# Smaller copies of the split values, and spare time ahead of four norm products, in a fused attention and MoE kernel

## The chip, the core and the metric

The kernel runs on one core of a Trainium2 chip. Times are device microseconds of one execution on that core. TensorE is called PE, VectorE DVE, ScalarE ACT, GpSimd POOL and SyncE SP, as in the profile. SP computes nothing here; it issues the copies and transposes that this text speaks of.

## The reference

Causal block attention, then two feed-forward stages without biases, all on float32 inputs.

```
B, H, S, D = 4, 8, 576, 64
scores = (q @ k.T) / sqrt(D)                   # per head
scores = where(i // 64 >= j // 64, scores, -1e9)
attn = softmax(scores)                         # with 1e-9 added to the sum
x = (attn @ v) as [2304, 512]

a, b = x @ w1, x @ w2                          # [2304, 1024]
x = ((a * b) @ w3) @ w_out                     # [2304, 512]

r = maximum(x @ w_in, 0)                       # [2304, 2048]
out = (r * r) @ w_out2
```

## The kernel before

Float32 products are made of 16-bit ones: an operand is split into an upper part (fp16, "h") and a remainder (fp16, "l"), and three products stand for one. Other operands (g, w3·w_out, the later q and k) are split into two fp32r parts in the same way.

**Attention** works on pairs of heads, p = 0 to 15, two heads on the two halves of the 128 partitions, and on query tiles t = 0 to 4 in three groups g. For each group the scores go to a PSUM buffer `s` (L917 on PE; pairs 3 to 7 in float32 on `kraw,qraw`, later ones on split `qk`), DVE takes the row maxima `nm` (L951, L959), ACT the exponentials `pf` (L976), DVE the reciprocals `r`, and ACT and DVE the split weights `p` (L1020, L1027). SP then transposes `p` into `pt` by DMA (L1037). `attend` multiplies `pt` with the values in two parts (`attend 0` and `attend 1` of a pair, L1112) and ACT and DVE split the result into `x..h` and `x..l` (L1128, L1133).

Causality comes in blocks of 64 keys. So `attend` needs the values not only as `split_v` makes them (`v16`, five blocks of 128 keys) but also shifted by 64 keys (`vsh`) and with blocks that are mixed from two (`vmix`). Both are copies from SBUF to SBUF that SP issues (L863), four for each pair from pair 3 on: `mixb` 0, `mixb` 1, `s0`, `s1`. The shifted copies hold upper and lower parts; `attend` reads their upper parts alone (`for hl in range(1 if w is sh else 2)`).

**The first MoE stage** follows batch by batch behind attention and fills PE between its steps. `ab_products` (L1208) makes a and b from x in 12 products for each of 8 tiles f of w1/w2, ACT scales a (L1363), DVE multiplies (L1370), and g = a·b is split. `y_products` multiplies g with the product w3·w_out; ACT evicts y (`ys`, L1413) and POOL stores it. ab and y take turns in three PSUM banks of 512 columns, so an ab product may wait until ACT has evicted the y that had its bank.

w1/w2's eight tiles f are converted from 64-bit words and scaled by a power of two before they are split: `w12_tile` sums squares of each half on ACT (`junk`, L431) or takes maxima on DVE (`wsum`, L424), `norm_scale` multiplies these sums by a matrix of ones on PE to spread them over all partitions (L375, a product of 2 columns into `pv_bank`), and DVE makes the scale's exponent from that (L381, L283) for the split (L302, L305). The same helper serves two other norms, with n = 1.

**The second MoE stage** (from about 500 us on) uses Strassen's products on split operands; no line of it is changed.

**Order.** Nothing of this is issued where it is written. Each step is recorded with an engine, a modelled cost, what it reads and writes, a key and a spare time:

```
def op(self, eng, cost, fn, r=(), w=(), key=0.0, spare=0.0):
```

`emit` then plans the whole program: on each engine it takes the step that can start earliest, and of those that can start by then the one with the smallest key. A step can start when its producers are done by the model; from another engine that is

```
u.ready = max(u.ready, free[eng] + u.same if same else o.end + self.WAIT + u.spare)
```

So `spare` holds a step back in the plan: others pass it. A DMA's cost is a triple: 0.6 us of issue on SP or POOL, its length in KB times 0.0033 us in one shared pipe, and 4.0 us until it has landed:

```
def c_dma(kb):
    return (0.6, kb * 0.0033, LATE)
```

The plan is fixed when the program is built. On the chip each engine works through its own queue in the planned order and waits on semaphores for what is really done.

Of the kernel before, what the change touches and what calls it, by code (L numbers as in the profile page):

```python
# [10 lines left out]
F16 = mybir.dt.float16  # L11
# [3 lines left out]
AF = mybir.ActivationFunctionType  # L15
ALU = mybir.AluOpType
# [3 lines left out]
P = 128  # L20
# [9 lines left out]
NTILE = 5  # L30
# [50 lines left out]
class Order:  # L81
# [14 lines left out]
    def buf(self, pool, tag, bufs, shape, dtype, name):  # L96
        b = Buf(self, pool, tag, bufs, shape, dtype, name)
        self.bufs.append(b)
        return b
# [88 lines left out]
def fused_kernel(ctx: ExitStack, tc: tile.TileContext, qT, kT, vp, va, w12, w3t, wo, wb, out):  # L188
    nc = tc.nc
    act, dve, pe, sp, pool = nc.scalar, nc.vector, nc.tensor, nc.sync, nc.gpsimd  # L190
    ctx.enter_context(tc.manual_schedule())

    od = Order()
    buf = od.buf

    PE, ACT, DVE, SQ, GQ = "P", "A", "V", "S", "G"
# [16 lines left out]
    def c_dma(kb):  # L213
        return (0.6, kb * 0.0033, LATE)
# [154 lines left out]
    def norm_scale(n, col, sums, sum_keys, scale, inverse, key):  # L369


        bank = norm_cols[0]
        od.op(
            PE, 0.06,
            lambda: pe.matmul(bank()[:, NB + col : NB + col + n], upper(ones, 0, P), upper(sums, 0, n), start=True, stop=True),  # L375
            [(ones,)] + sum_keys, [(bank, col)], key,
        )
        h = at_buf("nh", 2, [P, 2], I32, f"nh_{col}")
        od.op(
            DVE, c_dve(8),  # L380
            lambda: dve.tensor_scalar(  # L381
                out=h()[:, :n], in0=bank().bitcast(I32)[:, NB + col : NB + col + n], scalar1=24, scalar2=None,
                op0=ALU.logical_shift_right,
            ),
            [(bank, col)], [(h,)], key,
        )
        od.op(DVE, c_dve(8), lambda: bits(scale(), h()[:, :n], -1.0, 204.0), [(h,)], [scale.key], key)
        od.op(DVE, c_dve(8), lambda: bits(inverse(), h()[:, :n], 1.0, 50.0), [(h,)], [inverse.key], key)
# [181 lines left out]
    def at_buf(tag, bufs, shape, dtype, name):  # L570
        return buf("at", tag, bufs, shape, dtype, name)
# [11 lines left out]
    vals = {}  # L583
# [217 lines left out]
    def split_v(p):  # L801

        key = 2 * p * HEAD + 2
        src = raws[p][2]
        first = p < KDM
        one = p < 2 * KDM
        sc = None if one else vsc[2 * p // H][0]
        t = at_buf("vraw" if first else "v16", 2, [P, NTILE, 2, P], F16, f"v16_{p}")  # L810
        wide = (NTILE + NTILE - 1) * 2 * P
        if first:
            slot = (5, 6)[p - KDM]
            mixb = sh_ = buf("base", f"w8_{slot}", 1, [P, wide], F16, f"vmix_{p}")
        else:
            mixb = buf("cv", "raw", RAW_BUFS, [P, 512], I64, f"vmix_{p}")
            sh_ = buf("cv", "cx", 2, [P, NTILE - 1, 2, P], F16, f"vsh_{p}")

        def mix():
            m = mixb() if first else mixb().bitcast(F16)  # L820
            return m[:, : NTILE * 2 * P].rearrange("p (c h x) -> p c h x", c=NTILE, h=2)

        def sh():
            if not first:
                return sh_()
            return sh_()[:, NTILE * 2 * P :].rearrange("p (c h x) -> p c h x", c=NTILE - 1, h=2)

        if one:
            sx = x_scale[2 * p // H][0]

            def joined_heads():
                return src().rearrange("p c a d -> p c (a d)")

            split_scaled(
                lambda: t()[:, :, 0, :], lambda: t()[:, :, 1, :], joined_heads, 640,
                ([(t, "h", a) for a in range(2)], [(t, "l", a) for a in range(2)], [(src,)]), (sx, [sx.key]), key,
            )
        for a in range(0 if one else 2):
            n = (2 * p + a) % H
            cols = slice(D * a, D * a + D)  # L840
            od.op(
                ACT, c_act(320),
                lambda a=a, n=n, cols=cols: act.activation(
                    t()[:, :, 0, cols], src()[:, :, a, :], AF.Copy, scale=sc()[:, n : n + 1]
                ),
                [(src,), (sc,)], [(t, "h", a)], key,
            )
            od.op(
                DVE, c_dve(320),
                lambda a=a, n=n, cols=cols: dve.scalar_tensor_tensor(  # L850
                    out=t()[:, :, 1, cols], in0=src()[:, :, a, :], scalar=sc()[:, n : n + 1],
                    in1=t()[:, :, 0, cols], op0=ALU.mult, op1=ALU.subtract,
                ),
                [(src,), (sc,), (t, "h", a)], [(t, "l", a)], key,
            )
        whole = [(t, x, a) for x in "hl" for a in range(2)]
        for w, o, i in (
            ((mixb, 0), lambda: mix()[0:64], lambda: t()[0:64]),
            ((mixb, 1), lambda: mix()[64:128], lambda: t()[0:64, 0:1].broadcast_to([64, NTILE, 2, P])),
            ((sh_, "s0"), lambda: sh()[0:64], lambda: t()[64:128, : NTILE - 1]),  # L860
            ((sh_, "s1"), lambda: sh()[64:128], lambda: t()[0:64, 1:]),
        ):
            od.op(SQ, c_dma(190), lambda o=o, i=i: sp.dma_start(out=o(), in_=i()), whole, [w], key)  # L863
        vals[p] = t, mix, sh, whole + [(mixb, 0), (mixb, 1), (sh_, "s0"), (sh_, "s1")]

    def pair(p):

# [207 lines left out]
    def attend(p, part):  # L1075

        b = 2 * p // H
        key = (2 * p + 1) * HEAD + 6 + part
        c0, gn = GS[part]
        pv = pv_bank[0]  # L1080
        if whole(p):
            attend_whole(p, part, pv)
            return
        v, mix, sh, v_keys = vals[p]
        lo_t, hi_t = PARTS[part]
        todo = []
        for kind, w in ((0, v), (1, sh)):
            for c in range(hi_t):
                tiles = [t for t in (lo_t, hi_t) if c < t]
                if GROUP_OF[lo_t] == GROUP_OF[hi_t]:  # L1090
                    todo.append((w, c, tiles, [PT_BASE[t] + c + kind * (t + 1) for t in tiles]))
                else:
                    todo += [(w, c, [t], [PT_BASE[t] + c + kind * (t + 1)]) for t in tiles]
        todo += [(mix, t, [t], [PT_BASE[t] + t]) for t in (lo_t, hi_t)]
        if part == 0:
            todo.append((mix, 0, [0], [PT_BASE[0]]))
        steps = [(w, c, tiles, o, hl) for w, c, tiles, o in todo for hl in range(1 if w is sh else 2)]

        def products(lo, hi):
            for n in range(lo, hi):  # L1100
                w, c, tiles, o, hl = steps[n]
                for a in range(2):
                    pt = pts[2 * p + a, GROUP_OF[tiles[0]]]
                    rows = slice(64 * a, 64 * a + 64)
                    nq = 64 if tiles == [0] else 128
                    dst = pv()[rows, q_start(tiles[0]) - c0 : q_start(tiles[-1]) + nq - c0]
                    if len(tiles) == 2:
                        dst = dst.rearrange("p (t x) -> p t x", x=P)
                        rhs = pt()[:, o[0] : o[1] + 1 : o[1] - o[0], :]
                    else:  # L1110
                        rhs = pt()[:, o[0], :nq]
                    pe.matmul(dst, w()[:, c, hl, rows], rhs, start=n == 0, stop=n == len(steps) - 1)  # L1112

        pt_ks = [k for a in range(2) for g in ((0, 1) if part == 0 else (1, 2)) for k in pt_keys[2 * p + a, g]]
        cost = sum(c_mm(128 * len(s[2])) for s in steps)
        od.op(PE, cost + 0.2, lambda: products(0, len(steps)), v_keys + pt_ks, [(pv, "pv")], key, spare(p))
        xh, xl = x_part(p, part)
        kc = p % KDM
        if b > 1:
            t_back = vsc[b][1]  # L1120
            backs = [(t_back, 0), (t_back, 1)]

        def back():
            return t_back()[:, kc : kc + 1] if b > 1 else 2.0**-PEXP

        od.op(
            ACT, c_act(gn, 0.05),
            lambda: act.activation(xh(), pv()[:, :gn], AF.Copy, scale=back()),  # L1128
            [(pv, "pv")] + (backs if b > 1 else []), [(xh,)], key,
        )  # L1130
        od.op(
            DVE, c_dve(gn, 0.06),
            lambda: dve.scalar_tensor_tensor(  # L1133
                out=xl(), in0=pv()[:, :gn], scalar=back(), in1=xh(),
                op0=ALU.mult, op1=ALU.subtract,
            ),
            [(pv, "pv"), (xh,)] + (backs if b > 1 else []), [(xl,)], key,
        )
# [1323 lines left out]
```

## Time and profile before

| | |
|---|---|
| median of 3 runs | 834.83 us (833.37 to 835.41) |
| the profiled execution's own time | 834.87 us |
| its span, first to last instruction | 833.1 us |
| granted TensorE clock, mean | 0.997 of full speed |
| PE, weight load on PE, DVE, ACT, POOL busy | 815.8, 661.4, 707.3, 612.4, 103.4 us |

Busy is the union of an engine's instructions. PE's weight loads overlap its products. The span leaves out what lies before the first and behind the last instruction, 1.77 us of the execution's time.

### The profile page before, as it was taken

Reading aid. Unit: us, or ns where it says so; the run is one execution under the profiler, and the core shown is the slowest. Engines: PE = TensorE matmul, PEld = TensorE weight load, DVE = VectorE, ACT = ScalarE, POOL = GpSimd, SP = SyncE. Lnnn points to the kernel's source line nnn. Section 1 sums busy time; section 2 is a strip of 40 time slices with the busy share of each in tenths; the row PEclk is TensorE's granted clock in tenths of the full one; section 3 lists DMA queues with packets and bytes.
Section 4 is the critical chain, followed back from the end, with each engine's and each line's share of the span. In section 5 each row is a group of like instructions: output and inputs, shape, how many; then the busy total and the mean of one; then the engine's idle time right before and its main releaser. Section 6 shows DMA issues by size and latency. Waiting matters only on the chain.

```text
span 833.1 us, 18899 instructions
## 1 busy us (share of the span) xinstructions
PE 815.8 (98%) x7282; PEld 661.4 (79%) x7286; DVE 707.3 (85%) x1640; ACT 612.4 (74%) x1399; POOL 103.4 (12%) x190
## 2 busy tenths in 40 slices
PE   8999999999999999999999999999999999999997
PEld 7456777789779898798879887666678888888886
DVE  5999889988888998837787889999979898787775
ACT  5999988966886888847999967575756655673652
POOL 5021110112111012011313101100020000001000
PEclk9999999999999999999999999999999999999999
DMA  8856757789998899664746401120030011001001
GB/s 331 323 205 189 171 153 162 184 178 236 189 184 176 169 181 198 130 129 136 238 142 234 152 15 64 53 75 2 1 127 1 2 39 39 2 1 52 1 2 52
DMA packets 111739, 102.42 MB, mean 123 GB/s; under 512 B 89440, under 2 KB 93600, under 8 KB 110240
## 3 DMA queue, kind: packets, MB, share of 16 engines
q0 software_dynamic: 17888, 71.18, 26.3%
q1 hardware_dynamic: 93760, 30.03, 20.1%
q8 instruction: 57, 0.93, 0.5%
q14 instruction: 34, 0.28, 0.1%
HBM read 62.78 MB, written 9.44 MB: 87 GB/s over the span
## 4 chain that ended last, share of the span: by engine, by line
PE 52%; DVE 10%; ACT 4%; issue 1%; DVEq 0%; ACTq 0%
PE p L1987 14%; PE ab L1208 13%; PE p L2155 11%; PE y L1208 6%; PE o L2282 5%; PE pv_bank L1112 2%; PE s L917 1%; DVE t L2110 1%; DVE s L1930 1%; DVE c L2019 1%; ACT c L2050 1%; DVE g L295 1%; ACT c L2053 1%; DVE gs L295 1%; DVE ts L2132 1%
## 5 line engine op out<-in xcount | busy, mean ns | idle before, releaser
L1208 PEld LDWEIGHTS <-w 128*128 128x128 f16 x1536 | 147.0, 98 | 43.7 <-issue 6.8
L976 ACT ACTIVATE pf<-s,nm 128x192 f32<-128x192 f32 (+4 forms) x160 | 83.3, 536 | 38.5 <-DVE nm L959 33.0
L1208 PE MATMUL ab<-x0h,w 128*128 128x320 f16 x512 | 109.8, 299 | 0.7 <-ACT ys L1413 0.7
L1208 PE MATMUL y<-g,w3o 128*128 128x320 f32 (+1 forms) x768 | 109.5, 299 | 0.0
L1208 PEld LDWEIGHTS y<-g,w3o 128*128 128x128 f32 x768 | 103.3, 188 | 2.0 <-issue 1.1
L1208 PE MATMUL ab<-x1h,w 128*128 128x256 f16 x512 | 88.1, 273 | 1.3 <-ACT ys L1413 1.3
L2155 PEld LDWEIGHTS <-gs 128*128 128x128 f16 x816 | 79.5, 98 | 10.4 <-DVE gs L295 1.3
L1987 PEld LDWEIGHTS <-wb 128*128 128x128 f16 x768 | 75.1, 98 | 12.1 <-issue 0.5
L1208 PE MATMUL ab<-x0l,w 128*128 128x320 f16 x256 | 76.5, 299 | 0.0
L1027 DVE SCALAR_TENSOR_TENSOR p<-pf,r,p 128x192 f16<-128x192 f32 (+4 forms) x130 | 67.4, 546 | 4.4 <-ACT p L1020 3.7
L1208 PE MATMUL ab<-x1l,w 128*128 128x256 f16 x256 | 69.8, 272 | 0.0
L1020 ACT ACTIVATE p<-pf,r 128x192 f16<-128x192 f32 (+4 forms) x130 | 67.3, 569 | 1.9 <-DVE r L993 1.2
L2282 PE MATMUL o<-wb,g 128*128 128x512 f16 x288 | 66.3, 379 | 0.3 <-DVE c L2292 0.2
L2050 ACT ACTIVATE c<-c,beta 128x512 f32<-128x512 f32 x48 | 34.3, 714 | 43.5 <-DVE c L2019 43.5
L1987 PEld LDWEIGHTS <-st 128*128 128x128 f16 x576 | 56.3, 98 | 7.2 <-issue 0.3
L2155 PE MATMUL p<-ts,gs 128*128 128x256 f16 x480 | 61.6, 273 | 0.1
L2282 PEld LDWEIGHTS <-g 128*128 128x128 f16 x288 | 28.0, 98 | 30.0 <-issue 0.5
L2155 PE MATMUL p<-wb,gs 128*128 128x256 f16 x336 | 44.7, 273 | 0.1
L293 ACT ACTIVATE gs<-c 128x512 f16<-128x512 f32 (+1 forms) x56 | 29.9, 535 | 18.3 <-DVE c L2061 18.1
L951 DVE TENSOR_REDUCE nm<-s 128x2 f32<-128x384 f32 (+1 forms) x64 | 42.1, 684 | 1.0
L356 DVE CUSTOM_DVE_ANT_0 cx<-raw,cx 128x1024 uint16<-128x1024 uint16 (+1 forms) x53 | 39.1, 738 | 2.9 <-ACT raw L347 0.7
L261 ACT ACTIVATE g<-a 128x320 fp32r<-128x320 f32 (+1 forms) x64 | 28.2, 441 | 16.0 <-DVE a L1370 15.5
(287 smaller groups left out, 1988.7 us busy)
## 6 DMA issues: line engine op xcount, KB each, us to landing
raw<-in_wb POOLq DMA_DIRECT2D x32, 512.0 KB, 5.5
raw<-in_w3t POOLq DMA_DIRECT2D x8, 1024.0 KB, 10.1
raw<-in_w POOLq DMA_DIRECT2D x16, 512.0 KB, 4.9
yraw<-ydram POOLq DMA_DIRECT2D x12, 512.0 KB, 4.2
vraw<-in_vp POOLq DMA_DIRECT2D x16, 320.0 KB, 4.7
qraw<-in_qT POOLq DMA_DIRECT2D x16, 288.0 KB, 4.0
kraw<-in_kT POOLq DMA_DIRECT2D x16, 288.0 KB, 5.1
vmix<-v SPq DMA_DIRECT2D x26, 160.0 KB, 4.8
```

The lines of the kernel that those rows point to most:

```text
L261: od.op(ACT, c_act(n), lambda: act.activation(hi(), src(), AF.Copy), [ks], kh, key)
L293: od.op(ACT, c_act(n), lambda: act.activation(hi(), src(), AF.Copy), ks, kh, key)
L356: dve.tensor_tensor(out=x(), in0=x(), in1=words()[1], op=ALU.add)
L951: lambda k=k, t=t, nm=nm, banks=banks: dve.tensor_reduce(out=nm()[:, k], in_=banks[0]()[:, :, S_COL[t] : S_COL[t] + n_keys(t)], op=ALU.max ...
L976: act.activation(o, view(a, t), AF.Exp, bias=nm()[:, k, a : a + 1], scale=SCALE, accum_out=ssum()[:, k, a : a + 1],)
L1020: lambda o=o, nk=nk, a=a, k=k, w=weights, p16=p16, r=r: act.activation(p16()[:, o : o + nk], w(a, k), AF.Copy, scale=r()[:, k, a : a + 1]),
L1027: lambda o=o, nk=nk, a=a, k=k, w=weights, p16=p16, r=r: dve.scalar_tensor_tensor(out=p16()[:, o + nk : o + 2 * nk], in0=w(a, k), scalar=r( ...
L1208: pe.matmul(acc(), l, r, start=k == 0, stop=k == len(mms) - 1)
L1987: pe.matmul(acc()[:, TH * half : TH * half + TH], lhs(a, kc), y[yn]()[:, kc], start=n == 0, stop=n == len(mms) - 1,)
L2050: lambda src=src, k=k: act.activation(src(), src(), AF.Relu, scale=beta()[:, j, k : k + 1]),
L2155: pe.matmul(acc()[:, TH * u : TH * u + TH], t()[:, o : o + P], r(b), start=first and n == 0 and u == tiles[0], stop=last and n == 2 and u ...
L2282: pe.matmul(o(), g[gx]()[:, cols], wt(f)[:, a, 512:1024], start=(begin and n == 0), stop=(last and n == 2),)
```

## The change

Two edits. The first is in `split_v` and in the two places that read its tiles. The split values `v16` are laid out as upper half, then lower half, instead of block by block; the shifted copies `vsh` hold the upper half alone (64 KB each instead of 128); the second mixed copy is issued in two (upper 80 KB, lower 80 KB). The shifted copies and one of the mixed ones need only the upper parts of v to be done. Where each of four copies was planned with 190 KB, the five are planned with 64, 64, 160, 80 and 80, and the shifted ones come first. The second edit gives `norm_scale`'s product a spare of 1.1 us where n is 2 and col at least 8, that is for tiles f = 4 to 7 of w1/w2.

```
 def norm_scale(n, col, sums, sum_keys, scale, inverse, key):
...
-            [(ones,)] + sum_keys, [(bank, col)], key,
+            [(ones,)] + sum_keys, [(bank, col)], key, 1.1 * (n == 2 and col >= 8),
...
 def split_v(p):
...
-        t = at_buf("vraw" if first else "v16", 2, [P, NTILE, 2, P], F16, f"v16_{p}")
-        wide = (NTILE + NTILE - 1) * 2 * P
+        t = at_buf("vraw" if first else "v16", 2, [P, 2, NTILE, P], F16, f"v16_{p}")
+        wide = (3 * NTILE - 1) * P
...
-            sh_ = buf("cv", "cx", 2, [P, NTILE - 1, 2, P], F16, f"vsh_{p}")
+            sh_ = buf("cv", "cx", 2, [P, NTILE - 1, P], F16, f"vsh_{p}")
...
-            return m[:, : NTILE * 2 * P].rearrange("p (c h x) -> p c h x", c=NTILE, h=2)
+            return m[:, : NTILE * 2 * P].rearrange("p (h c x) -> p h c x", h=2, c=NTILE)
...
         whole = [(t, x, a) for x in "hl" for a in range(2)]
-        for w, o, i in (
-            ((mixb, 0), lambda: mix()[0:64], lambda: t()[0:64]),
-            ((mixb, 1), lambda: mix()[64:128], lambda: t()[0:64, 0:1].broadcast_to([64, NTILE, 2, P])),
-            ((sh_, "s0"), lambda: sh()[0:64], lambda: t()[64:128, : NTILE - 1]),
-            ((sh_, "s1"), lambda: sh()[64:128], lambda: t()[0:64, 1:]),
+        upper_ = [(t, "h", a) for a in range(2)]
+        for w, o, i, kb, ks in (
+            ((sh_, "s0"), lambda: sh()[0:64], lambda: t()[64:128, 0, : NTILE - 1], 64, upper_),
+            ((sh_, "s1"), lambda: sh()[64:128], lambda: t()[0:64, 0, 1:], 64, upper_),
+            ((mixb, 0), lambda: mix()[0:64], lambda: t()[0:64], 160, whole),
+            ((mixb, 1), lambda: mix()[64:128, 0], lambda: t()[0:64, 0, 0:1].broadcast_to([64, NTILE, P]), 80, upper_),
+            ((mixb, 2), lambda: mix()[64:128, 1], lambda: t()[0:64, 1, 0:1].broadcast_to([64, NTILE, P]), 80, whole),
         ):
-            od.op(SQ, c_dma(190), lambda o=o, i=i: sp.dma_start(out=o(), in_=i()), whole, [w], key)
+            od.op(SQ, c_dma(kb), lambda o=o, i=i: sp.dma_start(out=o(), in_=i()), ks, [w], key)
...
-                    pe.matmul(dst, w()[:, c, hl, rows], rhs, start=n == 0, stop=n == len(steps) - 1)
+                    x = w()[:, c, rows] if w is sh else w()[:, hl, c, rows]
+                    pe.matmul(dst, x, rhs, start=n == 0, stop=n == len(steps) - 1)
```

The plan is made anew from these costs, so most of the order behind the first changed copy moves a little. PE has 11768 rows in either program; SP has 122 before and 128 now, one row standing for two equal issues where they follow each other. Line numbers behind the edit are 2 or 3 higher in the changed kernel.

On PE, at the sums of w1/w2's last tile (`wsum_7`), the end of one ab group, the norm product, and the scores of pair 5's last group stood so before:

```order
L1208 MATMUL ab_0_0_6_0_2056<-x0h3_0_1351,w12_3_1959 128x320
L375 LDWEIGHTS ones_89
L375 MATMUL pv_bank_356<-wsum_7_2064,ones_89 128x2
L917 MATMUL s_5_2_0_2087<-kraw_5_1223,qraw_5_1216 128x288
L917 MATMUL s_5_2_1_2089<-kraw_5_1223,qraw_5_1216 128x288
L917 MATMUL s_5_2_0_2087<-kraw_5_1223,qraw_5_1216 128x288
L917 MATMUL s_5_2_1_2089<-kraw_5_1223,qraw_5_1216 128x288
L1208 LDWEIGHTS w12_3_1959
L1208 MATMUL ab_0_0_6_1_2106<-x0h0_0_461,w12_3_1959 128x320
```

and stand so now:

```order
L1211 MATMUL ab_0_0_6_0_2059<-x0h3_0_1352,w12_3_1975 128x320
L919 MATMUL s_5_2_0_2087<-kraw_5_1224,qraw_5_1217 128x288
L919 MATMUL s_5_2_1_2089<-kraw_5_1224,qraw_5_1217 128x288
L919 MATMUL s_5_2_0_2087<-kraw_5_1224,qraw_5_1217 128x288
L919 MATMUL s_5_2_1_2089<-kraw_5_1224,qraw_5_1217 128x288
L375 LDWEIGHTS ones_89
L375 MATMUL pv_bank_356<-wsum_7_2067,ones_89 128x2
L1211 LDWEIGHTS w12_3_1975
L1211 MATMUL ab_0_0_6_1_2103<-x0h0_0_461,w12_3_1975 128x320
```

The norm product has moved behind the four rows of scores (eight products, a row here being what the program wrote for both heads' halves); those of tiles 4 to 6 have moved behind six ab products each in the same way.

On SP, the end of pair 8's transposes and the copies of pair 9 stood so before:

```order
L1037 DMA_TRANSPOSE pt_8_2_0_3353<-p16_8_2_0_3330 128x9x128
L863 DMA vmix_9_3380<-v16_9_3309 64x1280
L863 DMA vmix_9_3380<-v16_9_3309 64x5x256
L863 DMA vsh_9_3394<-v16_9_3309 64x1024 x2
L1037 DMA_TRANSPOSE pt_8_2_1_3435<-p16_8_2_1_3391 128x9x128
```

and now:

```order
L1039 DMA_TRANSPOSE pt_8_2_0_3345<-p16_8_2_0_3327 128x9x128
L1039 DMA_TRANSPOSE pt_8_2_1_3410<-p16_8_2_1_3384 128x9x128
L865 DMA vsh_9_3435<-v16_9_3398 64x512 x2
L865 DMA vmix_9_3448<-v16_9_3398 64x1280
L865 DMA vmix_9_3448<-v16_9_3398 64x5x128 x2
L1039 DMA_TRANSPOSE pt_9_0_0_3523<-p16_9_0_0_3458 128x8x128
```

Pair 8's last transpose has moved ahead of the copies; the copies are five, the shifted ones first and of half the length, and the one that repeats a block in two.

On PE, at the end of the third group of y with the scores of pair 11, the rows before (`y_1_0_3` is batch 1, first part of its columns, block 3 of the outputs; `ab_1_1_0_0` batch 1, second part, tile f = 0, w1; `s_11_1` pair 11, group 1), from inside these scores to the first ab product behind y:

```order
L917 MATMUL s_11_1_4077<-qk0_11_3680,qk1_11_3700 128x448 x2
L917 MATMUL s_11_1_4077<-qk0_11_3680 128x64 x2
L917 MATMUL s_11_1_4077<-qk1_11_3700,qk0_11_3680 128x64 x2
L917 MATMUL s_11_1_4077<-qk0_11_3680,qk1_11_3700 128x64 x2
L1208 MATMUL y_1_0_3_4028<-g_1_0_0_3211,w3o_1_742 128x320 x6
L1208 MATMUL y_1_0_3_4028<-g_1_0_4_3507,w3o_2_1005 128x320 x6
L1208 MATMUL y_1_0_3_4028<-g_1_0_4_3507,w3o_3_1246 128x320 x6
L1208 LDWEIGHTS w12_0_980
L1208 MATMUL ab_1_1_0_0_4133<-x1h0_1_2290,w12_0_980 128x256
```

and now, from the end of the same scores on:

```order
L919 MATMUL s_11_1_4029<-qk1_11_3781,qk0_11_3706 128x64 x2
L919 MATMUL s_11_1_4029<-qk0_11_3706,qk1_11_3781 128x64 x2
L1211 MATMUL y_1_0_2_3937<-g_1_0_0_3208,w3o_1_742 128x320 x6
L1211 MATMUL y_1_0_2_3937<-g_1_0_4_3506,w3o_2_1006 128x320 x6
L696 MATMUL pv_bank_356<-vdiag_3_3891,ones_89 128x128
L1211 MATMUL y_1_0_2_3937<-g_1_0_4_3506,w3o_3_1247 128x320 x6
L1211 MATMUL y_1_0_3_4099<-g_1_0_0_3208,w3o_0_509 128x320 x6
L1211 MATMUL y_1_0_3_4099<-g_1_0_0_3208,w3o_1_742 128x320 x6
L1211 MATMUL y_1_0_3_4099<-g_1_0_4_3506,w3o_2_1006 128x320 x6
L1211 MATMUL y_1_0_3_4099<-g_1_0_4_3506,w3o_3_1247 128x320 x6
L1211 LDWEIGHTS w12_0_982
L1211 MATMUL ab_1_1_0_0_4154<-x1h0_1_2283,w12_0_982 128x256
```

The scores of pair 11 have moved ahead of 24 more of y's products. In both programs 24 ab products of `ab_1_1_0` follow; then came `ab_1_1_1_0`, and now the first `attend` of pair 10 stands ahead of it.

## Rows read from the trace of the kernel before

**Rows 1.** the page: the span, and busy time of each engine.

```profile
span 833.1 us, 18899 instructions
...
PE 815.8 (98%) x7282; PEld 661.4 (79%) x7286; DVE 707.3 (85%) x1640; ACT 612.4 (74%) x1399; POOL 103.4 (12%) x190
```

**Rows 2.** windows of 20 us: window, length, busy us (x instructions), PEclk, DMA share, GB/s.

```profile
120.00:140.00 20.00, 19.21 (x157) 14.61 (x156) 19.65 (x50) 17.28 (x38) 3.65 (x7) 1.00 0.55 164
140.00:160.00 20.00, 17.92 (x146) 13.78 (x144) 18.86 (x57) 17.32 (x47) 1.84 (x4) 1.00 0.93 176
260.00:280.00 20.00, 18.69 (x210) 16.75 (x209) 16.97 (x49) 13.67 (x41) 3.26 (x6) 1.00 1.02 228
520.00:540.00 20.00, 19.49 (x135) 12.97 (x133) 20.00 (x42) 10.92 (x23) 1.96 (x4) 1.00 0.15 50
```

**Rows 3.** waits of PE: line, releaser, us in total, times, longest.

```profile
PE pv_bank L375 <- ACT junk L431: 2.3, 3, 1.3
PE ab L1208 <- ACT ys L1413: 2.0, 2, 1.3
...
PE pv_bank L375 <- DVE wsum L424: 0.8, 2, 0.5
```

**Rows 4.** timeline of PE: start, us, engine, line, out<-in, [idle before <-releaser].

```profile
128.80 0.16 PE L375 MATMUL pv_bank<-wsum,ones 128*128 128x2 bf16 x1 [0.54 <-DVE wsum L424]
128.83 0.30 PE L1208 MATMUL ab<-x0h,w 128*128 128x320 f16 x1
128.96 0.30 PE L1208 MATMUL ab<-x0l,w 128*128 128x320 f16 x1
...
138.72 0.16 PE L375 MATMUL pv_bank<-wsum,ones 128*128 128x2 bf16 x1 [0.24 <-ACT junk L431]
...
148.17 0.16 PE L375 MATMUL pv_bank<-wsum,ones 128*128 128x2 bf16 x1 [1.25 <-ACT junk L431]
...
158.00 0.16 PE L375 MATMUL pv_bank<-wsum,ones 128*128 128x2 bf16 x1 [0.83 <-ACT junk L431]
158.09 1.24 PE L917 MATMUL s<-kraw,qraw 64*128 64x288 f32 x8
```

**Rows 5.** timeline of ACT at the third of these products.

```profile
147.38 0.65 ACT L431 ACTIVATE junk<-cx 128x512 bf16<-128x512 f32 x1
147.90 0.22 ACT L431 ACTIVATION_READ_ACCUMULATOR junk<-cx 128x1 f32 x1
```

**Rows 6.** timeline of PE at three later places.

```profile
214.47 0.30 PE L1208 MATMUL ab<-x0h,w 128*128 128x320 f16 x1 [0.69 <-ACT ys L1413]
...
244.90 0.97 PE L1112 MATMUL pv_bank<-pt,v 128*64 128x128 f16 x28
...
275.40 0.27 PE L1208 MATMUL ab<-x1h,w 128*128 128x256 f16 x1 [1.29 <-ACT ys L1413]
```

**Rows 7.** timeline of ACT ahead of the last of these.

```profile
272.52 0.42 ACT L976 ACTIVATE pf<-s,nm 128x192 f32<-128x192 f32 x1 [2.93 <-DVE nm L959]
...
274.91 0.44 ACT L1413 ACTIVATE ys<-y 128x320 f32<-128x320 f32 x1
```

**Rows 8.** timeline of SP's queue, issues joined by the line (x of them).

```profile
230.80 1.14 SPq L863 DMA_DIRECT2D vmix<-v  x2
...
233.77 7.87 SPq L1037 DMA_TRANSPOSE pt<-p  x3
```

**Rows 9.** the page: packets, DMA queues (packets, MB, share of 16 engines), issues.

```profile
DMA packets 111739, 102.42 MB, mean 123 GB/s; under 512 B 89440, under 2 KB 93600, under 8 KB 110240
...
q1 hardware_dynamic: 93760, 30.03, 20.1%
...
vmix<-v SPq DMA_DIRECT2D x26, 160.0 KB, 4.8
```

**Rows 10.** the tile pt: from issue to landing.

```profile
DMA to landing us min/median/max: 3.0/4.4/8.0
```

**Rows 11.** the tile vsh: from issue to landing.

```profile
DMA to landing us min/median/max: 2.3/4.5/8.4
```

More of the change, by code (lines that the diff above doesn't have):

```diff
@@ L825, in sh @@
                 return sh_()
-            return sh_()[:, NTILE * 2 * P :].rearrange("p (c h x) -> p c h x", c=NTILE - 1, h=2)
+            return sh_()[:, NTILE * 2 * P :].rearrange("p (c x) -> p c x", c=NTILE - 1)
         if one:
@@ L834, in split_v @@
             split_scaled(
-                lambda: t()[:, :, 0, :], lambda: t()[:, :, 1, :], joined_heads, 640,
+                lambda: t()[:, 0], lambda: t()[:, 1], joined_heads, 640,
                 ([(t, "h", a) for a in range(2)], [(t, "l", a) for a in range(2)], [(src,)]), (sx, [sx.key]), key,
@@ L843, in split_v @@
                 lambda a=a, n=n, cols=cols: act.activation(
-                    t()[:, :, 0, cols], src()[:, :, a, :], AF.Copy, scale=sc()[:, n : n + 1]
+                    t()[:, 0, :, cols], src()[:, :, a, :], AF.Copy, scale=sc()[:, n : n + 1]
                 ),
@@ L850, in split_v @@
                 lambda a=a, n=n, cols=cols: dve.scalar_tensor_tensor(
-                    out=t()[:, :, 1, cols], in0=src()[:, :, a, :], scalar=sc()[:, n : n + 1],
-                    in1=t()[:, :, 0, cols], op0=ALU.mult, op1=ALU.subtract,
+                    out=t()[:, 1, :, cols], in0=src()[:, :, a, :], scalar=sc()[:, n : n + 1],
+                    in1=t()[:, 0, :, cols], op0=ALU.mult, op1=ALU.subtract,
                 ),
@@ L856, in split_v @@
         whole = [(t, x, a) for x in "hl" for a in range(2)]
-        for w, o, i in (
-            ((mixb, 0), lambda: mix()[0:64], lambda: t()[0:64]),
-            ((mixb, 1), lambda: mix()[64:128], lambda: t()[0:64, 0:1].broadcast_to([64, NTILE, 2, P])),
-            ((sh_, "s0"), lambda: sh()[0:64], lambda: t()[64:128, : NTILE - 1]),
-            ((sh_, "s1"), lambda: sh()[64:128], lambda: t()[0:64, 1:]),
-        ):
-            od.op(SQ, c_dma(190), lambda o=o, i=i: sp.dma_start(out=o(), in_=i()), whole, [w], key)
-        vals[p] = t, mix, sh, whole + [(mixb, 0), (mixb, 1), (sh_, "s0"), (sh_, "s1")]
+        upper_ = [(t, "h", a) for a in range(2)]
[5 more added lines that the diff above has]
+            ((mixb, 2), lambda: mix()[64:128, 1], lambda: t()[0:64, 1, 0:1].broadcast_to([64, NTILE, P]), 80, whole),
+        ):
+            od.op(SQ, c_dma(kb), lambda o=o, i=i: sp.dma_start(out=o(), in_=i()), ks, [w], key)
+        vals[p] = t, mix, sh, whole + [(mixb, 0), (mixb, 1), (mixb, 2), (sh_, "s0"), (sh_, "s1")]
     def pair(p):
```

## The prediction

> **What bounds the kernel now.** I read the page first: PE is busy for 815.8 of 833.1 us [rows 1], so all that a reordering can give back lies in the 17 us in which PE does nothing, and part of that is the load of the first data and the tail. The table of 20 us stretches says where the rest is: 0.8 us are missing in 120 to 140, 2.1 in 140 to 160, 1.3 in 260 to 280 and 0.5 in 520 to 540 [rows 2]; most stretches between them are full. PE's waits say who ends them: the small product of L375 three times ACT's L431 (2.3 us) and twice DVE's L424 (0.8), the ab products twice the eviction of y at L1413 (2.0) [rows 3]. No line of that view names a DMA as the one that ended a wait of PE. So a copy that lands sooner buys nothing by itself; what can buy something is a PE instruction that no longer stands first in its queue while its input is unfinished.
>
> Four of those stand in the timeline: L375 of w1/w2's tiles 4 to 7 waits 0.54, 0.24, 1.25 and 0.83 us, 2.86 together [rows 4]. The third shows the mechanism: ACT's two halves of the last Square run from 147.38 to about 148.12 [rows 5], PE's product starts at 148.17, and ACT did not idle ahead of it: its queue is full. That matters below: the product is early, but ACT is also late.
>
> **The spare.** In the planned order tiles 4 and 5's L375 go behind six ab products of 320 columns, tile 6's behind six of 256, tile 7's behind the eight score products of pair 5. In the trace one ab product of 320 takes 0.13 us from start to start (128.83 to 128.96), the eight score products 1.24 [rows 4]. Six products are 0.8 us; of 256 columns, by the share of columns, 0.62 (estimate). If ACT and DVE delivered at the same moments as before, the four waits would shrink to 0, 0, 0.63 and 0: a gain of 2.23; with tile 6's Square coming 0.7 us earlier too, as its place in ACT's new order suggests, the whole 2.86, the upper bound. The lower bound is 0: the work behind the product is the same in sum, and if PE only arrives sooner at the next thing that ACT or DVE owes it, the waits move. ACT and DVE are busy 17.28 and 19.65 of 20 us in the first stretch, 17.32 and 18.86 in the second [rows 2]; neither is full for the whole of it, but DVE is within 2% in the first. So I take about half of the upper bound: **-1.4**. What stands behind L375 on DVE are its exponent steps and then the splits of w; those come later than before by what L375 is moved, 0.6 to 1.2 us, and their reader, the ab products of that tile, stands some ten us behind: nothing on the path.
>
> **The smaller copies.** The shifted copies lose half of their bytes and one mixed copy is split: five issues instead of four per pair, 448 KB instead of 576. PE does the same products, since the shifted copies were only ever read in their upper parts. What it costs: one more issue on SP, about 0.74 us (four issues of pair 9 stand between 230.80 and 233.77 [rows 8]), and smaller pieces in the mixed copy that repeats one block: 64 x 5 pieces of 512 bytes become two times 64 x 5 of 256, 320 packets more. The packets between 512 bytes and 2 KB are 93600 less 89440 [rows 9], 4160, which is 13 pairs of 320, so the pieces are packets. q1's 93760 packets took 20.1% of 16 engines' 833.1 us, 28.6 ns each [rows 1, 9]; 320 x 28.6 ns / 16 = 0.57 us of flight, against which 128 KB fewer stand. Whether either shows depends on the slack of the attends. The tightest that I found is pair 8's second: its last transpose is issued from 233.77 on, behind the four copies of pair 9, and the slowest transpose lands 8.0 us after issue [rows 8, 10], so by 241.8; PE reads it at 244.90 [rows 6]: 3.1 us to spare, more than 0.74 + 0.57. The copies are issued by 233.77 and land at most 8.4 us later [rows 8, 11], by 242.2, and their first reader stands behind 244.90. So both edits cost **0**; without that cover it would be up to 1.3 us for each pair. At this place the new order does two things: the attend stands 24 products closer behind its scores, 3.1 us at 0.13 each [rows 4], which would use up the slack; and its transpose stands ahead of the copies of pair 9 instead of behind them, which gives 2.97 us back [rows 8]. I count that as even; it is where the third rival would bite first.
>
> A rule speaks against the change. In the trace the mixed copies of 160 KB land after 4.8 us and the shifted ones of 128 KB after 4.5 [rows 9, 11]: a fifth of the bytes is worth 0.3 us, and the bytes saved here at most 1 us of flight. The Trainium skill ("DMA: Bandwidth & Descriptors", section Specifications) says that a transfer needs at least 512 bytes for line rate, and that below it the engine reads, modifies and writes; by that rule the copies cut to 256 bytes would land later than the one they replace, and the transposes queued behind them too. By the row the sum holds; by the rule it holds as long as 3.1 us cover it, and past that it is the third rival.
>
> **What the new costs do to the plan.** The planner reckoned with four copies of 190 KB and now with 64, 64, 160, 80 and 80, so that the copies seem to be done sooner; from pair 8 on the scores and attends stand earlier by 2 to 4 us of MoE products (counted in the order at the rates of [rows 4]). I followed the places where PE waits now.
>
> At 275.40 ab waits 1.29 us for its bank [rows 6]: the eviction of y at 274.91 stands on ACT behind pair 11's first exps, and these start at 272.52 after 2.93 us of waiting for the maxima [rows 7]. In the changed order pair 11's scores stand ahead of 24 more of y's products, and the attend of pair 10 has come in between ab_1_1_0_1 and the ab that waits. The exps then start earlier and the eviction is not late: **-1.3** (bounds: 0, if the maxima are late again, and -1.46, the gap from start to start). At 214.47 the wait of 0.69 [rows 6] is for an eviction too; one of the two evictions comes about 3 us earlier, the other 2 later behind four p of pair 8: the wait moves by one ab group, **0** (bounds -0.7 and +0.7). Late in the kernel DVE is full (20.00 of 20 in 520 to 540) and PE lacks 0.51 there [rows 2]; since attention ends some 2.6 us of MoE products sooner, the preparation of the second block starts sooner: **-0.3** (bounds 0 and -0.5).
>
> **Sum.** -1.4 + 0 - 1.3 + 0 - 0.3 = -3.0 us. The profiled execution took 834.87 for a span of 833.1, 1.77 around it, and lies 0.04 above the median of 834.83. 834.87 - 3.0 = 831.9.
>
> **The rivals.** *The waits only move* (rival 1). For it: ACT's Square at 147.38 was not waiting for anything, and DVE runs at 98% in 120 to 140 [rows 2, 5]; then what L375 gains is lost at the next eviction. Against it: PE is only short of 2.9 us in these 40. Then L375 gives 1.1, 0.4 comes back as score waits, and the wait at 275 reappears elsewhere: -0.7 and 0.1 for noise of the plan, 834.87 - 0.6 = 834.3.
>
> *Evictions of y behind the exps* (rival 2, the other side). From pair 8 on attention stands denser ahead of y's last products, and each time that y's bank is freed on ACT behind a group of exps, ab waits like at 275.40, 1.3 us [rows 6]. y is evicted in eight groups in the kernel, five of them within attention, each with a seam to the next ab. With five waits of 1.3 us, the old two gone (-2.0) and L375 giving 1.1: 834.87 - 1.1 - 2.0 + 6.5 = 838.3. It decides from three such waits on (3.1 gained against 3.9 lost). Against it: in the order I found one place of that kind, not five.
>
> *Small pieces* (rival 3). If transposes and copies fly more than 3.1 us longer, the attends wait in order of their slack; with 4.5 us more about five of them, together some 4 us: 831.9 + 4 = 835.9. For it speaks the rule above; against it, that no copy flew longer than 8.4 us [rows 11], though 89440 packets of 111739 are under 512 bytes already [rows 9].
>
> **How the numbers follow.** 0.3% of 834.83 is 2.5 us, about what a measurement of this kernel can tell from none: faster is below 832.3, slower above 837.3. Forecast 0.52, rival 1 0.32, rival 2 0.10, rival 3 0.06. The forecast's terms have bounds from -5.5 (2.86, 1.46, 0.7 and 0.5 together) to +0.7, and I give it 829.4 to 833.5; it lies on the faster side 7 times in 10, 0.37. Rival 1 adds 0.05 there and 0.27 to the same, rival 2 is two in three slower (0.07), rival 3 mostly the same. Faster 0.43, same 0.47, slower 0.10. The range reaches from the forecast's low end over rival 1 to rival 3: 829.4 to 836.0, with most of rival 2 and the forecast's tail left out.
>
> **What the profile of the changed kernel would show.** L375's waits for L431 and L424 fall from 3.1 us together to about 1.5, and the missing time of PE in 120 to 160 from 2.9 to 1.5. At the y to ab seam near 274 PE has no wait over 0.5 us. No attend of L1115 waits for a DMA. Copies land in 4 to 5 us. PE's busy time stays at 815 to 816 us. It is wrong if PE's missing time in 120 to 160 stays at 2.9 while L375 no longer waits (rival 1), if ab waits for ys at three or more places (rival 2), or if PE waits for pt or a copy (rival 3).

## The result and the profile after

The changed kernel takes 839.19 us (median of 18 runs, 835.04 to 844.96) against 834.90 before (18 runs, 833.35 to 836.48): a ratio of 1.0059, 95% interval 1.0042 to 1.0077. It is slower by about 0.6% (0.5% by the medians alone), and its runs lie 9.9 us apart where those of before lie 3.1 apart. The profiled execution is one of the long ones, 843.70 us with a span of 841.9. The prediction said 831.9 and a range of 829.4 to 836.0.

The page, as in [rows 1, 9]:

```profile
span 841.9 us, 18913 instructions
...
PE 818.7 (97%) x7282; PEld 661.5 (79%) x7286; DVE 709.2 (84%) x1640; ACT 611.7 (73%) x1399; POOL 102.8 (12%) x190
...
DMA packets 116107, 100.72 MB, mean 120 GB/s; under 512 B 97968, under 2 KB 99632, under 8 KB 114608
...
q1 hardware_dynamic: 98128, 28.33, 20.9%
```

For the same 7282 products PE is busy 2.9 us longer, and idle 23.2 us instead of 17.3: 8.8 us in all. The windows, as in [rows 2], and three of 4 us:

```profile
120.00:140.00 20.00, 19.90 (x161) 14.83 (x159) 19.62 (x50) 17.16 (x38) 3.52 (x7) 1.00 0.59 166
140.00:160.00 20.00, 18.85 (x155) 14.12 (x154) 18.86 (x57) 17.46 (x48) 2.71 (x5) 1.00 0.95 166
228.00:232.00 4.00, 2.73 (x21) 1.84 (x19) 0.00 (x0) 0.19 (x1) 0.00 (x0) 1.00 1.09 147
232.00:236.00 4.00, 1.70 (x8) 1.05 (x8) 3.29 (x7) 4.00 (x13) 0.00 (x0) 0.83 1.35 122
236.00:240.00 4.00, 4.00 (x24) 2.58 (x22) 3.43 (x9) 3.70 (x12) 0.58 (x2) 0.74 0.67 140
260.00:280.00 20.00, 20.00 (x234) 18.76 (x232) 16.95 (x48) 14.11 (x40) 2.18 (x4) 1.00 0.72 150
520.00:540.00 20.00, 19.61 (x142) 13.44 (x143) 20.00 (x40) 12.60 (x27) 0.70 (x1) 1.00 0.09 27
```

Where the gain was looked for it came: in 120 to 160 PE lacks 1.25 us instead of 2.87, and 260 to 280 is full. But from 228 to 232 nearly everything comes to a stand: DVE does nothing for 4 us, ACT works 0.19, and PE runs out of products at 230.73. PE's waits, as in [rows 3], and the line of ACT's waits that answers them, of the changed kernel and then of the one before:

```profile
PE ab L1211 <- ACT a L1366: 4.5, 2, 3.6
...
PE pv_bank L1115 <- DMA pt<-p: 1.7, 1, 1.7
PE ab L1211 <- DVE a L1373: 1.6, 3, 0.8
...
PE ab L1211 <- ACT ys L1416: 0.5, 1, 0.5
...
PE pv_bank L375 <- DVE wsum L424: 0.3, 1, 0.3
```

```profile
ACT p L1022 <- DMA pt<-p: 11.2, 3, 7.3
```

```profile
ACT p L1020 <- DMA pt<-p: 0.7, 1, 0.7
```

L375 waits 0.3 us for its sums where it had waited 3.1. In its place ab waits for ACT, and ACT, which waited 0.7 us for transposes before, waits 11.2. The timeline of ACT, then of PE, then of POOL shows the one wait of 7.33 us:

```profile
223.59 0.89 ACT L1022 ACTIVATE p<-pf,r 128x448 f16<-128x448 f32 x2
231.81 0.77 ACT L1022 ACTIVATE p<-pf,r 128x576 f16<-128x576 f32 x1 [7.33 <-DMA pt<-p]
...
233.72 0.52 ACT L1366 ACTIVATE a<-ab,ab_back 128x320 f32<-128x320 f32 x1
```

```profile
230.43 0.30 PE L1211 MATMUL ab<-x0h,w 128*128 128x320 f16 x1
234.30 0.30 PE L1211 MATMUL ab<-x0h,w 128*128 128x320 f16 x1 [3.57 <-ACT a L1366]
...
235.81 0.47 PE L1211 MATMUL ab<-x0l,w 128*128 128x320 f16 x1
```

```profile
218.33 0.54 POOL L648 DMA_DIRECT2D qraw<-in_qT  x1
218.91 0.54 POOL L651 DMA_DIRECT2D kraw<-in_kT  x1
219.64 0.54 POOL L672 DMA_DIRECT2D va<-in_va  x1 [0.19 <-issue]
```

The split weights `p` have four buffers, and a buffer is free when its transpose has read it. The transposes of pair 8's first group were issued at 218.54 and 219.98 and landed at 231.73 and 234.95: 13.2 and 15.0 us in flight, by which I mean the time from issue to landing. ACT stands in front of a `p` whose buffer the first of them holds; the scaling of a at 233.72 stands behind it in ACT's queue, ab's bank behind that. Then, after PE's idle 3.57 us, the granted clock is 0.83 and 0.74 in the two windows, a mixture of the levels 2.4 and 1.2 GHz, and one product of 320 columns takes 0.47 us instead of 0.30. The tile pt in the whole trace, for what was issued from 216 to 226 us, and for the same stretch of the kernel before:

```profile
DMA to landing us min/median/max: 3.0/4.8/15.0
```

```profile
DMA to landing us min/median/max: 4.1/11.7/15.0
```

```profile
DMA to landing us min/median/max: 4.9/7.6/7.8
```

Much of the rest is lost near 296 to 307 us, where a transpose flies 10.75: ACT waits for it again, and PE's attend 1.7 us.

### The profile page after: what moved, and what is told of

Same layout as the page of the kernel before. It is cut to its first block, busy times and chain, and to the rows that moved or that the text cites. A ratio compares the mean times of both kernels' runs of the same rounds, so it can differ in the third digit from the quotient of the medians.

```text
span 841.9 us, 18913 instructions
## 1 busy us (share of the span) xinstructions
PE 818.7 (97%) x7282; PEld 661.5 (79%) x7286; DVE 709.2 (84%) x1640; ACT 611.7 (73%) x1399; POOL 102.8 (12%) x190
## 4 chain that ended last, share of the span: by engine, by line
PE 49%; DVE 9%; ACT 4%; issue 1%; DVEq 0%; ACTq 0%
PE p L1990 14%; PE p L2158 11%; PE ab L1211 10%; PE y L1211 6%; PE o L2285 5%; DVE t L2113 2%; PE pv_bank L1115 1%; DVE c L2022 1%; ACT c L2053 1%; PE s L919 1%; DVE s L1933 1%; DVE ts L2135 1%; PE h L1894 1%; ACT c L2056 1%; DVE gs L295 1%
## 5 line engine op out<-in xcount | busy, mean ns | idle before, releaser
L1990 PEld LDWEIGHTS <-wb 128*128 128x128 f16 x768 | 75.1, 98 | 12.3 <-issue 0.7
L1022 ACT ACTIVATE p<-pf,r 128x192 f16<-128x192 f32 (+4 forms) x130 | 66.3, 563 | 12.5 <-DMA pt<-p 11.2
L295 DVE TENSOR_TENSOR gs<-c,gs 128x512 f16<-128x512 f32 (+1 forms) x56 | 32.2, 574 | 8.4 <-ACT gs L293 8.4
```

What stands on the lines that cost most here:

```text
L295: DVE, c_dve(n), lambda: dve.tensor_tensor(out=lo(), in0=src(), in1=hi(), op=ALU.subtract), kh + ks, kl, key
L1022: lambda o=o, nk=nk, a=a, k=k, w=weights, p16=p16, r=r: act.activation(p16()[:, o : o + nk], w(a, k), AF.Copy, scale=r()[:, k, a : a + 1]),
L1990: pe.matmul(acc()[:, TH * half : TH * half + TH], lhs(a, kc), y[yn]()[:, kc], start=n == 0, stop=n == len(mms) - 1,)
```

## The experiments

Theory A, formed from this trace: transposes that fly beside POOL's loads from HBM become late, and the new plan puts them there. Theory B: the pieces of 256 bytes slow the DMA queues. Theory C: the spare's order is the loss. Ratios are to the kernel before, measured beside each. The flights are those of one profiled execution of each kernel, whose own time is given; a kernel's other runs can have had others.

| kernel | us, median (range, runs) | ratio (95%) | pt's flight, median/max (profiled run) |
|---|---|---|---|
| changed | 839.19 (835.04 to 844.96, 18) | 1.0059 (1.0042 to 1.0077) | 4.8/15.0 (843.70) |
| e1 spare only | 833.64 (832.62 to 836.12, 12) | 0.9993 (0.9982 to 1.0004) | 4.5/8.7 (832.88) |
| e2 copies only | 838.39 (837.66 to 842.98, 6) | 1.0056 (1.0036 to 1.0076) | 4.1/10.3 (838.66) |
| e3 changed, old costs | 834.21 (832.28 to 835.78, 12) | 0.9991 (0.9981 to 1.0001) | 4.2/8.1 (835.61) |
| e4 old copies, new costs | 834.27 (833.20 to 838.81, 12) | 1.0000 (0.9986 to 1.0014) | 4.3/9.0 (833.29) |
| e5 changed, fills | 835.06 (834.79 to 836.57, 12) | 1.0002 (0.9993 to 1.0012) | 3.3/7.0 (834.82) |
| e6 before, fills | 834.60 (834.18 to 836.06, 12) | 0.9996 (0.9986 to 1.0006) | 3.5/7.3 (834.22) |
| e7 changed, whole pieces | 837.59 (834.69 to 839.63, 12) | 1.0029 (1.0014 to 1.0044) | 4.8/12.3 (839.31) |
| e8 changed, five p buffers | 837.96 (837.14 to 844.91, 12) | 1.0047 (1.0027 to 1.0067) | 4.4/10.2 (837.23) |
| e9 changed, late transposes | 841.12 (840.78 to 841.54, 5) | 1.0074 (1.0061 to 1.0087) | 4.2/11.8 (840.89) |
| e10 spare, late transposes | 845.25 (843.43 to 846.49, 4) | 1.0122 (1.0106 to 1.0137) | 4.5/15.0 (845.47) |
| e11 changed, va filled | 839.97 (836.03 to 842.39, 6) | 1.0057 (1.0036 to 1.0078) | 4.6/11.5 (842.39) |
| e12 changed, old sequence | 836.28 (834.82 to 842.63, 12) | 1.0029 (1.0012 to 1.0046) | 4.6/9.0 (835.76) |

**e1, the spare alone,** in the kernel before:

```
-            [(ones,)] + sum_keys, [(bank, col)], key,
+            [(ones,)] + sum_keys, [(bank, col)], key, 1.1 * (n == 2 and col >= 8),
```

> The kernel before with the spare of 1.1 us alone. Theory A (transposes that fly beside POOL's loads from HBM crawl, and the new plan of the copies puts them there): the spare alone gives what the four waits of L375 cost, 832 to 834 us, with the spread of the kernel before (3 us). Theory B (pieces of 256 bytes slow the DMA queues): the same, 832 to 834. Theory C (the spare's new order itself is the loss): 838 to 840.

833.64 us, 1.2 below before, with an interval that still holds 1: C falls. The waits of L375 for the sums are gone, and others have come. The waits of PE from 120 to 380 us:

```profile
PE s L917 <- ACT pf L976: 2.3, 2, 1.4
PE ab L1208 <- DVE a L1370: 1.1, 2, 0.7
PE y L1208 <- DVE a L1370: 0.4, 1, 0.4
```

That is 3.8 us, where the kernel before has 4.8 in the same stretch.

**e2, the copies alone:** the changed kernel without that line's spare.

> The changed copies and their new modelled costs, without the spare. A and B: slower than the kernel before by about as much as the whole change and more, 838 to 842 us, with its wide spread (8 us or more between the runs). C: 833 to 836.

838.39: the loss belongs to the first edit.

**e3, the changed kernel with the old sum of costs:**

```
-            od.op(SQ, c_dma(kb), lambda o=o, i=i: sp.dma_start(out=o(), in_=i()), ks, [w], key)
+            od.op(SQ, c_dma(152), lambda o=o, i=i: sp.dma_start(out=o(), in_=i()), ks, [w], key)
```

> The whole change, but the plan reckons each of the five copies with 152 KB, so that a pair's copies cost the plan 760 as before. A: the transposes keep their distance from the loads, 833 to 836 us, spread under 4 us, no transpose over 10 us of flight. B: the pieces are still there, 838 to 842.

834.21: as A said. The small pieces are all there, SP's queue stands almost as in the changed kernel, and no transpose of the profiled run flew over 8.1 us. B falls as the whole cause.

**e4, the old copies with the new sum of costs** (and the spare):

```
-            od.op(SQ, c_dma(190), lambda o=o, i=i: sp.dma_start(out=o(), in_=i()), whole, [w], key)
+            od.op(SQ, c_dma(112), lambda o=o, i=i: sp.dma_start(out=o(), in_=i()), whole, [w], key)
```

> The copies of the kernel before (four, 576 KB, pieces of 512 bytes), with the spare, reckoned with 112 KB each, 448 in all as in the changed kernel. A: the plan is too early for the flights, 838 to 842 us and a wide spread. B: the old pieces fly as before, 832 to 835.

834.27, a miss of A as I had put it: the sum of the modelled costs does not by itself make the loss. How near this plan is to the changed one can be counted in the traces, by operation, tile names without numbers, and shape: 44 of PE's 7282 products, 19 of DVE's 1640 operations, 19 of ACT's 1399 and 1 of POOL's 190 stand elsewhere than in the changed kernel; against the kernel before it is 654, 504, 392 and 5. So e4 is nearly the changed order with the old copies, and it loses nothing in the median (one run of 12 took 838.81). The same copies in another order (e3) lose nothing either. It takes the new copies and this order together. From here on I kept the order where I could and took causes out of it.

**e5, the changed order without the loads;** q, k and v of pairs 8 to 15 and `va` of batches 2 and 3 are filled by POOL instead:

```
-        od.op(GQ, c_dma(288), lambda: pool.dma_start(out=q(), in_=qT[p]), after, [(q,)], key)
+        od.op(GQ, c_dma(288), lambda: pool.memset(q(), 0.1) if p >= 8 else pool.dma_start(out=q(), in_=qT[p]), after, [(q,)], key)
```

and so for k, v and va; no other row of any queue differs.

> The changed kernel with every queue in the same order, word for word, but the loads of q, k and v of pairs 8 to 15 and of va for batches 2 and 3 are fills with a constant on POOL, so that these bytes don't come from HBM and the output is not the reference's. Theory A (transposes beside POOL's loads crawl, and this plan puts a burst of loads beside three transposes near 219 us): no transpose above 6 us of flight behind 200 us, no wait of ACT for pt there, the time 831 to 834 us and the spread of its runs under 3 us. Theory B (pieces of 256 bytes, or SP's longer queue): still 837 to 841 us with a spread of 6 us or more.

**e6, the same in the kernel before.**

> The same replacement of loads by fills in the kernel before, as the control: what the loads cost there and what the fills on POOL cost. A: 833 to 835 us, since no transpose was late there, so that the changed kernel without loads stands 1 to 3 us below it. B: 833 to 835 as well, with the changed one 3 to 6 us above it.

835.06 and 834.60. Without the loads the changed order is 4.1 us faster than with them, its runs lie 1.8 us apart instead of 9.9, and no transpose issued between 160 and 380 us flies over 5.9 us (view of the tile, e5):

```profile
DMA to landing us min/median/max: 3.0/3.3/5.9
```

In the kernel before the same replacement is worth 0.3 us. So the loads beside the transposes are the loss, in this order. And the two orders, both rid of it, are 0.5 us apart, the changed one not the faster: the forecast's 3 us are missing too, and e5 misses the 831 to 834 us that A gave it. PE's waits from 120 to 380 us, of e5 and then of e6:

```profile
PE ab L1211 <- DVE a L1373: 1.6, 3, 0.8
PE s L919 <- ACT pf L978: 1.2, 3, 0.6
PE ab L1211 <- ACT a L1366: 1.0, 1, 1.0
PE ab L1211 <- ACT ys L1416: 0.5, 1, 0.5
PE y L1211 <- DVE a L1373: 0.2, 1, 0.2
```

```profile
PE pv_bank L375 <- ACT junk L431: 2.3, 3, 1.3
PE ab L1208 <- ACT ys L1413: 2.0, 2, 1.3
PE pv_bank L375 <- DVE wsum L424: 0.6, 1, 0.6
PE s L917 <- ACT pf L976: 0.3, 1, 0.3
PE pv_bank L696 <- DVE x1l L1133: 0.2, 1, 0.2
```

4.5 against 5.4 us. From 100 to 600 us PE lacks 6.4 us in e5 (493.57 of 500 busy) and 6.7 in e6 (493.31).

**e7, the changed order with larger pieces;** the two copies that repeat a block read five blocks in a row (and for `[0:64, 1, 0:1]` likewise):

```
-            ((mixb, 1), lambda: mix()[64:128, 0], lambda: t()[0:64, 0, 0:1].broadcast_to([64, NTILE, P]), 80, upper_),
+            ((mixb, 1), lambda: mix()[64:128, 0], lambda: t()[0:64, 0], 80, upper_),
```

> The changed kernel with every queue in the same order, but the two copies that repeat one block read five blocks in a row instead, so that their pieces are 1280 bytes and not 256; the mixed copies hold other values and the output is not the reference's. A: still 837 to 841 us, spread 6 us or more, transposes over 9 us near 219. B: 832 to 835.

837.59, between the two. No queue's order differs, and the blocks that are filled otherwise meet only the remainders of the split weights, so what differs for the queues is the pieces. The longest flight is 12.3 us and ACT still waits 8.0 us in p:

```profile
ACT p L1022 <- DMA pt<-p: 8.0, 2, 4.4
```

Transposes are late without the small pieces, too. The pieces may add to it: the interval (1.0014 to 1.0044) just overlaps the changed kernel's (1.0042 to 1.0077), none of 12 runs is over 840 us, and 8 of the changed kernel's 18 are. Up to some 1.6 us of the 4.3 may be theirs; that stays open.

**e8, five buffers for p** (`P_BUFS = 5`).

> The changed kernel with five buffers for the split weights p instead of four, planned anew. If the loss comes to PE through ACT, which stands in p's queue until a late transpose gives a buffer back: 832 to 836 us even if transposes are late. If PE itself waits for pt in attend, or the late transposes hit elsewhere: 837 or more.

837.96: in the profiled run, one of the short ones (its 12 runs reach 844.91), ACT no longer waits for pt at all, but this is a new plan too, and PE lacks 2.4 us in 200 to 240, waiting now for `x0l` and `ys` (1.3 and 0.8 us). The remedy at the place of the wait did not bring the time back.

**e9, the plan reckons transposes 2 us later,** in the changed kernel, **and e10,** in the kernel before with the spare:

```
-                    SQ, (1.25, 0.22 * blocks, LATE),
+                    SQ, (1.25, 0.22 * blocks, LATE + 2.0),
```

> The whole change, but the plan reckons 2 us more until a transpose has landed (6 us instead of 4), so that what reads pt, and what needs p's buffers again, stands later. Theory A (the loss is that transposes beside POOL's loads take 8 to 15 us where the plan left room for less): 833 to 836 us and a spread under 5 us, ACT's wait in p for pt under 2 us. If collisions cost the same wherever the plan puts them: 837 or more.

> The kernel before with the spare and with the same 2 us more for transposes in the plan; its copies are the old ones. A: transposes were not late there, so nothing to win: 832.5 to 835 us, as the spare alone.

841.12 and 845.25: both misses of A, and e9 lies where its other case stood. The later plan loses elsewhere: PE lacks 3.0 us in 100 to 120 alone, 0.7 in the kernel before (e10, as [rows 2]):

```profile
100.00:120.00 20.00, 17.01 (x162) 12.83 (x161) 15.93 (x41) 16.70 (x44) 3.41 (x6) 0.94 0.55 146
```

and it does not keep transposes and loads apart. In e10 the copies and their pieces are the old ones, and ACT waits all the same:

```profile
ACT p L1020 <- DMA pt<-p: 7.4, 3, 4.6
```

with a flight of 15.0 us. So late transposes need neither the new copies nor their pieces: in another order the old copies have them as well.

**e11, the changed order with only va filled.**

> The changed kernel with every queue in the same order, but only the six loads of va (384 KB each) for batches 2 and 3 are fills with a constant on POOL; q, k and v are loaded. If the third load of the burst near 219 us is what makes transposes late there: the flights over 10 us near 219 go, 836 to 838 us. If two loads are enough: no change, 838 to 841.

839.97: the time did not change; the profiled run, the longest of six, lost it at another place. Of what was issued from 216 to 226 us no transpose flies over 6.4 us now (15.0 before), and PE lacks 1.0 us in 200 to 240 instead of 4.6. In 280 to 320, where no va is loaded in either kernel, it lacks 4.3 (3.4 in the changed kernel), and the longest flight of the trace, 11.5 us, starts at 292.83:

```profile
200.00:240.00 40.00, 39.01 (x449) 32.05 (x448) 33.71 (x80) 31.57 (x89) 8.18 (x14) 1.00 1.00 194
280.00:320.00 40.00, 35.69 (x435) 31.70 (x433) 33.53 (x86) 30.23 (x88) 4.00 (x8) 1.00 0.97 143
```

So without va the place near 219 was spared here, and elsewhere q, k and v are enough. That va is what makes transposes late near 219, and that the place differs from run to run, is not shown by one profile of each.

**e12, the five copies in the old sequence,** mixed ones first, all waiting for `whole`; PE's and ACT's orders nearly those of the changed kernel.

> The changed kernel with its five copies in the old sequence (mixed ones first, all waiting for the lower part too); PE's and ACT's orders are nearly those of the changed kernel (48 and 16 lines of difference). If it matters that the shifted copies leave early and so leave the transposes alone with the loads: 833 to 836 us. If it is the order of the other queues: 837 to 841.

836.28, with single runs up to 842.63: between my two cases, nearer to the first. With the copies in the old sequence more than half of the median's loss is gone, by the ratio half. The longest flight of the profiled run, one of the short ones, is 9.0 us.

Over all kernels with loads I counted, for the 888 transposes issued behind 100 us, how many of POOL's transfers were in flight at some moment of theirs (worked out from the issue and landing times of the traces):

```
POOL's transfers   transposes   median flight   longest
0                  182          3.3             5.3
1                  223          3.7             9.6
2                  136          4.5             8.2
3                  161          4.7             11.7
4 and more         186          6.3             15.0
```

With none of POOL's transfers the copies hardly matter: 3.3 us beside none, 3.5 beside three or more (longest 4.9).

The company makes long flights possible, but it does not fix them. In the changed kernel the transpose of 13.2 us was issued 0.21 us behind the load of q, 0.37 ahead of that of k and 1.10 ahead of that of va. In e12 one stands at 0.22, 0.36 and 1.10 from the same three loads and flies 8.8 us; in e4 two stand about them (216.04 and 217.45, the loads at 216.53, 217.10 and 217.90) and fly 5.2 and 7.2. The kernel before, too, has two transposes (218.94 and 220.86) close behind the same loads (216.35 to 217.64), at 7.8 and 7.6 us. What was issued from 216 to 226 us in e12, then in e4:

```profile
DMA to landing us min/median/max: 5.8/6.4/8.8
```

```profile
DMA to landing us min/median/max: 3.2/4.3/7.2
```

## Why the prediction was wrong

**The spare, -1.4: right at its place.** PE lacks 1.6 us less in 120 to 160, and L375's waits fell by 2.8. Alone (e1) it is worth 1.2 us, not clear of noise. The first rival was right about what follows: of these 1.6 us PE lost 0.5 again in 160 to 200, where before it lacked nothing.

**The place at 275, -1.3: right.** 260 to 280 is full; in e5, which is not shifted by the lost time before it, PE lacks 0.4 us in 240 to 280 where it lacked 1.3. At the seam near 214 a wait for ys of 0.5 us stands instead of 0.69, as the sum's 0 said.

**The second MoE stage, -0.3: wrong in sign.** In 500 to 600 PE lacks 1.4 us in the changed kernel and 1.2 in e5, 0.8 before.

**What the sum left out** is the price of new waits elsewhere. Rid of the loads, the changed order has 1.4 us of new waits in 280 to 320 (38.63 of 40 busy, 40.00 before), and in all PE lacks as much as before: 6.4 us in 100 to 600. I had summed the waits that the order takes away and priced only those new ones that I found by following queues at the old places. The first rival, 834.3 us, describes this part: e5 stands 0.5 us above e6, whose intervals overlap.

**The step that failed: "both edits cost 0 in flight", on a slack of 3.1 us.** It took the longest flight of the old trace, 8.0 us, as the longest there is. The flight depends on what flies beside the transpose: it is 11.7 to 15.0 us where three transposes start between 218.5 and 224.1 with three loads that start between 218.3 and 219.6, and without the loads (e5) at most 5.9 between 160 and 380. I followed the queues of SP, PE, ACT and DVE in the new order, each by itself, and never set SP's against POOL's. Yet the place of the issues alone would not have given the number away, since transposes in the same company flew 5.2 to 8.8 us in the kernel before, e4 and e12. I also looked at attend as the only reader of a transpose. The reader that waited most was ACT, for the buffer that the transpose reads, and behind ACT stood DVE and PE.

**The second rival's** 838.3 us lies nearest to the measured time, by luck: ab waits for an eviction of y once, for 0.5 us, and not five times.

**The third rival** had the mechanism's place, "transposes and copies fly more than 3.1 us longer", and the wrong reason, small pieces; at 835.9 us it was also priced too low, since it counted the attends' waits and neither ACT's buffer nor the clock. The Trainium skill ("DMA: Bandwidth & Descriptors", section Specifications) asks for at least 512 bytes for line rate. That bears on the loss at most with the part that e7 leaves open, and e3 has all the small pieces and loses nothing. Another sentence of it speaks to what happened: "Trainium Kernel Development and Optimization", section Key Constraints, says that DMAs from SP, ACT and POOL run on the same 16 engines and interleave, and that issuing from several engines saves only the time of issuing. The table above agrees: 3.3 us beside none of POOL's transfers, 6.3 beside four or more.

What stays open: what makes the same company fly 5 to 9 us in one kernel and 11 to 15 in another, and which part of the new copies (their number, length, pieces or sequence) matters for it. In nearly one order the old four copies take 834.27 us (e4), five in the old sequence 836.28 (e12), five in the new one 839.19, and these without the loads 835.06 (e5).

## What to carry to other kernels

A planner with fixed flights can lose by a smaller transfer: here the new copies and the new order lose only together, and only beside the loads. Before a slack is counted as cover, ask what else will be in flight beside the transfer in the new order, and list every reader of a landing, the owner of the source buffer among them. A reordering's gain is the difference of all waits, old and new; the way to see it is to take a suspected cause out of an unchanged order (e5 and e6). A variant that is planned again (e8 to e10) changes more than its cause, so count first how far its order has moved: e4's had hardly moved, and that makes it one of the strongest runs here.

## What the runs showed of the hardware

A DMA transpose of 8 or 9 blocks of 128 by 128 lands after about 3.3 us with nothing from POOL beside it and after up to 15.0 beside loads of q, k and va from HBM; the loads suffer as well (kraw, issued at 218.91, landed at 230.80, 11.9 us; in the kernel before kraw's loads between 200 and 320 us take 6.2 in the median and at most 6.9). The DMA engines did not idle meanwhile: from 216 to 236 us they were occupied as much as before (share 1.17 against 1.15) and moved 142 GB/s instead of 244, before and then changed:

```profile
216.00:236.00 20.00, 20.00 (x219) 15.16 (x217) 18.26 (x46) 16.60 (x47) 4.03 (x8) 1.00 1.15 244
216.00:236.00 20.00, 15.96 (x165) 11.90 (x165) 13.38 (x32) 10.71 (x30) 2.16 (x4) 0.97 1.17 142
```

A wait of PE of 3.57 us was followed by a lower granted clock (0.83 and 0.74 in two windows of 4 us). By these two figures that is worth about 1.7 us (estimate: 17% and 26% of 4 us), part of the 2.9 us by which the same products took longer.
